# A transformer block on one core: the MLP's first product by 2 by 2 blocks with seven block products, token blocks in pairs

## The chip, the cores and the metric

The kernel runs on one core of a Trainium2 chip. The metric is the device time of one execution in microseconds (us), lower is better. Three runs of the kernel before took 2402.6, 2403.48 and 2406.64 us (median 2403.48).

The core's engines work side by side, each through its own instructions in the order of the program: TensorE (PE in the profile; PEld are its weight loads), VectorE (DVE), ScalarE (ACT), GpSimd (POOL) and SyncE (SP), which here issues all the DMAs.

## The reference

What is computed, cut to what matters (S = 2048 tokens, D = 576, 32 heads, F = 4608, all float32):

```python
x = A_x
mod = (_silu(c) @ w_mod).reshape(c.shape[0], 6, 1, -1)
sa, ca, ga, sb, cb, gb = (mod[:, 0], ..., mod[:, 5])
h = _layernorm(x) * (1 + ca) + sa
x = x + ga * _A_ref(h, A_wq, A_wk, A_wv, A_wo)     # 32 query heads, one k and v
h = _layernorm(x) * (1 + cb) + sb
y = _layernorm(h)
h = gelu(y @ w1 + b1)                              # [2048, 576] x [576, 4608]
x = x + gb * (h @ w2 + b2)                         # [2048, 4608] x [4608, 576]
```

## The kernel before

**Numbers.** Most matmuls take operands of type float32r, which keeps only part of a float32's bits. So each operand is split in two: hi is the value copied to float32r, lo is the value minus hi. A product is then three matmuls: hi by hi, hi by lo, lo by hi. The contraction over 576 rows has four blocks of 128 rows and a rest of 64. For the rest, the array has the 64 rows twice: the host stacks them, the lower copy is replaced by its lo part, and two matmuls with the hi and the lo of the other operand suffice. One block of 128 features by 512 tokens thus costs 4 x 3 + 2 = 14 matmuls of 512 columns.

**Stages.** The tokens lie in four blocks tb of 512, each of four tiles t of 128. Stage 1 makes q, k and v. Stage 2 runs the attention, 32 groups of four heads (n = 0 to 31, eight per token block), with the softmax's maxima, the scores, the exponentials and the product with V interleaved by a list written out by hand. A deque called fill holds generators for work on the side: the output projection of a block that is through (wo_block), its second layer norm (ln2_block). Each call of step(fill) runs one generator to its next yield. Stage 3 is the MLP. The instructions on each engine are in the order in which the Python code emits them; a yield is only a place at which the emitting code changes over to something else.

**Layer norm and operands.** ln2_tile (L513) normalizes one tile of 128 tokens, seven yields a tile in the MLP's first steps (blocks 2 and 3) and more in the attention (blocks 0 and 1). transpose_tile (L150) turns it over in PE into a psB buffer, ACT copies the hi part (L158) and DVE subtracts for the lo part (L159). The ten planes (five hi, five lo) of 128 x 512 lie in a tile Y[tb].

**MLP.** The features are in 18 groups of 256 (two blocks f of 128). A step is one group i and one token block tb. The list seq goes through the groups with blocks 0 and 1 for ten groups, with all four blocks for the eight others, then again through the first ten with blocks 2 and 3: 28 loads and splits of a group, 72 steps. Around a step:

- load_w (L733) loads W1's and W2's part of the group (640 and 576 KB); split_group (L743) splits them: ACT makes hi, POOL makes lo (DVE for the first groups) and multiplies W2 by half the gate. It yields between these pieces.
- fc1 (L763): per f the 14 matmuls into a psB buffer (proj, L232), then the GELU by its tanh form: ACT adds the bias (L776) and squares (L777), DVE multiplies (L778), ACT takes the tanh (L779), DVE multiplies (L781), ACT makes hi of the result, gh (L782), POOL its lo, gl (L783). It yields after the matmuls, after the tanh and at the end.
- fc2 (L786): per tile of 128 tokens 12 matmuls of 288 columns into one of two psA buffers, gh and gl standing, then DVE adds the result to XT (L802), which holds x and becomes the output.

The order within a step is the string "ma,tbt,sma,tbt,s": m and a are the matmuls and the first part of GELU, b its rest, t a tile of the second product of the step before, s a piece of split_group, and a comma a step of fill.

**Room.** psB has four buffers of one PSUM bank, psA two of two banks. The tag big has three buffers of 20 KB per partition (Y[0] to Y[2] and the attention's results in turn).

Of the kernel before, what the change touches and what calls it, by code (L numbers as in the profile page):

```python
# [15 lines left out]
NB = 4  # L16
TB = S // NB
NT = TB // 128
KD = 5
# [13 lines left out]
def block_kernel(ctx: ExitStack, tc, x, wqkv, wo, w1, b1, w2, b2, c, wmod, ident_in, out):  # L33
# [42 lines left out]
    pw = ctx.enter_context(tc.tile_pool(name="pw", bufs=1))  # L76
# [73 lines left out]
    def transpose_tile(Z, zt, t, k0, k1):  # L150
        p = psB()
        for k in range(k0, k1):
            tr(p[:, 128 * (k - k0):128 * (k - k0 + 1)], Z, k)
        n = k1 - k0
        src = p[:, :128 * n].rearrange("p (k c) -> p k c", k=n)
        hi = zt[:, k0:k1, 128 * t:128 * (t + 1)]
        lo = zt[:, KD + k0:KD + k1, 128 * t:128 * (t + 1)]
        ac.activation(hi, src, AF.Copy)  # L158
        ve.tensor_tensor(lo, src, hi.bitcast(F32), op=ALU.subtract)  # L159
# [325 lines left out]
    px = ctx.enter_context(tc.tile_pool(name="px", bufs=1, reuse_waits="tile"))  # L485
# [4 lines left out]
    WO, Y, ATT, B2 = {}, {}, {}, {}  # L490
# [22 lines left out]
    def ln2_tile(tb, t):  # L513
# [35 lines left out]
        transpose_tile(Z, Y[tb], t, 0, 4)  # L549
        yield  # L550
        transpose_tile(Z, Y[tb], t, 4, 5)
        yield

    def ln2_block(tb):
        if "b" not in B2:
            b2g = B2["b"] = px.tile([128, D], F32, name="b2g")
            sy.dma_start(b2g, b2.to_broadcast([128, D]))
            po.tensor_mul(b2g, b2g, BC[:, 2, :])
            po.tensor_scalar(b2g, b2g, 2.0, None, op0=ALU.mult)
        Y[tb] = big() if tb < 3 else pw.tile([128, 10, 512], F32R, name="y3", tag="wA", padded_shape=[128, 10, WQC])  # L560
        for t in range(NT):
            yield from ln2_tile(tb, t)

# [23 lines left out]
    def post_quad(n, PV):  # L587
# [23 lines left out]
        if qd < NQ - 1:  # L611
            for j in range(4):
                k, r = divmod(4 * qd + j, HC)
                sy.dma_start(A[DH * r:DH * (r + 1), :, k, :].bitcast(F32), os[32 * j:32 * j + DH].bitcast(F32))
        yield
# [69 lines left out]
    def between(n, kc):  # L685
# [8 lines left out]
        if kc == 1 and n >= 1 and n + 2 < NQT:  # L694
            load_q(n + 2)
        if kc == 8 and n % NQ == 0 and n:
# [28 lines left out]
    pv_mm(NQT - 1, 15, 0, 4)  # L725
    a2.__exit__(None, None, None)
# [4 lines left out]
    RAW, W, G = {}, {}, {}  # L731
    E = 10
    seq = [(i, (0, 1)) for i in range(E)] + [(i, (0, 1, 2, 3)) for i in range(E, NG)] + [(i, (2, 3)) for i in range(E)]  # L733
    final = {0: NG - 1, 1: NG - 1, 2: len(seq) - 1, 3: len(seq) - 1}

    def load_w(i):
        a = pm.tile([128, KD, 256], F32, name="w1r")
        b = pm.tile([128, 2, D], F32, name="w2r")
        sy.dma_start(a, w1[seq[i][0]])
        sy.dma_start(b, w2[seq[i][0]])  # L740
        RAW[i] = (a, b)

    def split_group(i):  # L743

        a, b = RAW.pop(i)
        h1 = pm.tile([128, KD, 256], F32R, name="w1h", bufs=2)
        l1 = pm.tile([128, KD - 1, 256], F32R, name="w1l", bufs=2)
        h2 = pm.tile([128, 2, D], F32R, name="w2h", bufs=2)
        l2 = pm.tile([128, 2, D], F32R, name="w2l", bufs=2)
        W[i] = (h1, l1, h2, l2)  # L750
        ac.activation(h1, a, AF.Copy)
        yield
        e = ve if i < 2 else po
        e.tensor_tensor(l1, a[:, :KD - 1], h1[:, :KD - 1].bitcast(F32), op=ALU.subtract)
        e.tensor_tensor(h1[64:, KD - 1], a[64:, KD - 1], h1[64:, KD - 1].bitcast(F32), op=ALU.subtract)
        yield
        (ve if i == 1 else po).tensor_tensor(b, b, BC[:, 2:3, :].to_broadcast([128, 2, D]), op=ALU.mult)
        yield
        ac.activation(h2, b, AF.Copy)
        po.tensor_tensor(l2, b, h2.bitcast(F32), op=ALU.subtract)  # L760
        yield

    def fc1(i, tb):  # L763

        h1, l1, _, _ = W[i]
        gh = pm.tile([128, 2, TB], F32R, name="gh", bufs=2)
        gl = pm.tile([128, 2, TB], F32R, name="gl", bufs=2)
        G[i, tb] = (gh, gl)
        for f in range(2):
            p = psB()  # L770
            proj(p, h1, l1, 128 * f, 128 * (f + 1), Y[tb])
            yield
            ft = 2 * seq[i][0] + f
            h = pm.tile([128, TB], F32, name="gx", bufs=2)
            s = px.tile([128, TB], F32, name="gs", tag="OT"[f])
            ac.activation(h, p, AF.Identity, bias=b1t[:, ft:ft + 1])  # L776
            ac.activation(p, p, AF.Square, bias=b1t[:, ft:ft + 1])  # L777
            ve.scalar_tensor_tensor(s, p, 1.0 / GA3, h, op0=ALU.add, op1=ALU.mult)  # L778
            ac.activation(p, s, AF.Tanh, scale=GC * GA3)  # L779
            yield  # L780
            ve.scalar_tensor_tensor(h, p, 1.0, h, op0=ALU.add, op1=ALU.mult)  # L781
            ac.activation(gh[:, f, :], h, AF.Copy)  # L782
            po.tensor_tensor(gl[:, f, :], h, gh[:, f, :].bitcast(F32), op=ALU.subtract)  # L783
            yield

    def fc2(i, tb):  # L786
        _, _, h2, l2 = W[i]
        gh, gl = G.pop((i, tb))
        for t in range(NT):
            p = psA()  # L790
            ts_ = slice(128 * t, 128 * (t + 1))
            for nn in range(2):
                cs = slice(288 * nn, 288 * (nn + 1))
                terms = []
                for f in range(2):
                    terms += [(gh[:, f, ts_], h2[:, f, cs]), (gh[:, f, ts_], l2[:, f, cs]),
                              (gl[:, f, ts_], h2[:, f, cs])]
                for q, (a, b) in enumerate(terms):
                    pe.matmul(p[:, nn, :288], a, b, start=(q == 0), stop=(q == len(terms) - 1))  # L799
            X = XT[:, NT * tb + t, :]  # L800
            Xv = X.rearrange("p (a b) -> p a b", a=2)
            ve.tensor_tensor(Xv, p[:, :, :288], Xv, op=ALU.add)  # L802
            if i == final[tb]:
                r0 = TB * tb + 128 * t
                sy.dma_start(out[r0:r0 + 128, :], X)
            yield

    load_w(0)
    wop = {(t, h2): (psC if t == 3 and h2 else psM if t < 2 and t + h2 < 2 else psB)()
           for t in range(NT) for h2 in range(2)}  # L810
    for t in range(NT):
        for h2 in range(2):
            wo_mm(NB - 1, t, h2, wop[t, h2], 0, KD - 1)
    for gen in posts:
        drain(gen)
    drain(split_group(0))
    for t in range(NT):
        for h2 in range(2):
            wo_mm(NB - 1, t, h2, wop[t, h2], KD - 1, KD)
            wo_add(NB - 1, t, h2, wop[t, h2])  # L820
    open_ps("3", 4)
    load_w(1)
    fill = deque([ln2_block(2), ln2_block(3)])
    steps = [(i, tb) for i in range(len(seq)) for tb in seq[i][1]]
    prev = None
    sp = iter(())
    for e, (i, tb) in enumerate(steps):
        if tb == seq[i][1][0]:
            drain(sp)
            W.pop(i - 2, None)  # L830
            if i + 1 < len(seq):
                sp = split_group(i + 1)
        if tb == 2:
            while fill:
                step(fill)
        f1 = fc1(i, tb)
        f2 = fc2(*prev) if prev else iter(())
        order = "ma,tbt,sma,tbt,s"
        if e == 0:
            order = "masbmab"  # L840
        elif e == 1:
            order = "mabmttsabtts"
        elif e == len(steps) - 1:
            order = "mabm,a,tbttt"
        for o in order:
# [56 lines left out]
```

## Time and profile before

| | |
|---|---|
| median of three runs | 2403.48 us |
| the profiled execution | 2401.06 us |
| its span | 2399.2 us |
| PE, DVE, ACT, POOL busy, share of the span | 98%, 71%, 71%, 32% |
| first matmul of the MLP | 1448.84 us |
| granted clock of PE | 0.999 |

The span is the time from the first to the last instruction that the profiler recorded. "Busy" is the time in which an engine executes; waiting is not counted. In lists of instructions the columns are start, length, engine, line, operation, out<-in, shapes, and in brackets the idle time just before with what ended it. In lists of groups they are line, engine, operation, count, then the busy time in us, the mean length in ns, and the idle time in front.

### The profile page before, as it was taken

To read this page: it belongs to the slowest core of one execution; us is meant where nothing else is said; L and a number is where in the kernel's file an instruction comes from. 1 tells how busy PE (TensorE), PEld (TensorE's weight loads), DVE (VectorE), ACT (ScalarE), POOL (GpSimd) and SP (SyncE) were. 2 spreads that over 40 slices of the span, in tenths; PEclk is the share of its full clock that TensorE was granted. 3 is DMA by queue.
4 is the path that set the end of the run, shared out by engine and by line. 5 is a ranking of instruction groups with operands and counts; after the bars stand their busy time and mean duration, and the time that the engine had idled before them with its cause. 6 is when DMAs were issued, how large, how long until landed. Compare 5 with 4: busy or idle time off the path is not lost.

```text
span 2399.2 us, 42867 instructions
## 1 busy us (share of the span) xinstructions
PE 2356.6 (98%) x16802; PEld 1492.0 (62%) x16802; DVE 1712.5 (71%) x3069; ACT 1691.8 (71%) x3170; POOL 766.4 (32%) x669
## 2 busy tenths in 40 slices
PE   8999999999999999999999999999999999999999
PEld 6643444454444444444544348888899899989988
DVE  6589999979999889999799926767444444444444
ACT  5469999979999889999799994444444444444443
POOL 6502211114331123321010113665543333345553
PEclk9999999999999999999999999999999999999999
DMA  6412000000000000000000001111100000011111
GB/s 216 139 64 71 18 23 22 14 19 22 19 21 19 17 19 22 19 22 14 14 22 19 18 28 53 42 52 42 53 22 31 21 22 22 26 67 52 44 52 50
DMA packets 40586, 91.86 MB, mean 38 GB/s; under 512 B 5835, under 2 KB 9547, under 8 KB 40385
## 3 DMA queue, kind: packets, MB, share of 16 engines
q1 hardware_dynamic: 40385, 89.13, 11.6%
q8 instruction: 132, 2.16, 0.4%
q14 instruction: 69, 0.57, 0.1%
HBM read 66.06 MB, written 14.16 MB: 33 GB/s over the span
## 4 chain that ended last, share of the span: by engine, by line
PE 87%; DVE 6%; ACT 4%; issue 1%; POOL 1%; DMA 1%; SPq 0%; POOLq 0%; ACTq 0%; DVEq 0%
PE psC L650 20%; PE psB L239 20%; PE psA L799 17%; PE psB L661 10%; PE psM L310 10%; PE psB L671 4%; PE psB L573 2%; ACT P L663 2%; DVE mx L683 1%; PE psB L148 1%; PE psA L310 1%; PE psB L194 1%; DVE XT L802 1%; DVE Z L532 1%; ACT O L592 0%
## 5 line engine op out<-in xcount | busy, mean ns | idle before, releaser
L663 ACT ACTIVATE P<-psB 128x512 f32<-128x512 f32 x2048 | 1049.9, 617 | 2.2 <-PE psB L661 1.1
L683 DVE TENSOR_REDUCE mx<-psM 128x1 f32<-128x512 f32 x1476 | 943.1, 683 | 47.5 <-PE psM L310 27.3
L650 PE MATMUL psC<-P,V 128*32 128x256 f32 (+1 forms) x6056 | 598.2, 466 | 12.1 <-ACT O L592 12.1
L310 PE MATMUL psM<-KS,qst 64*128 64x512 f32 x1722 | 596.9, 432 | 3.3 <-DVE mx L683 2.4
L661 PE MATMUL psB<-qst,KS 64*128 64x512 f32 x2048 | 598.0, 433 | 1.0 <-DMA qst<-ms 0.5
L778 DVE SCALAR_TENSOR_TENSOR gs<-psB,gx 128x512 f32<-128x512 f32 x144 | 99.6, 692 | 453.3 <-ACT psB L777 453.3
L661 PEld LDWEIGHTS psB<-qst,KS 64*128 64x128 f32 x2048 | 305.0, 184 | 166.5 <-issue 72.5
L310 PEld LDWEIGHTS psM<-KS,qst 64*128 64x128 f32 x1722 | 284.3, 184 | 127.7 <-DVE mx L681 79.5
L783 POOL TENSOR_TENSOR gl<-gx,gh 128x512 fp32r<-128x512 f32 x144 | 188.6, 1309 | 494.1 <-ACT gh L782 447.3
L799 PE MATMUL psA<-w2h,gl 128*128 128x288 f32 x1152 | 341.4, 296 | 3.2 <-POOL gl L783 3.2
L799 PE MATMUL psA<-w2h,gh 128*128 128x288 f32 x1152 | 340.2, 295 | 1.9 <-ACT gh L782 1.5
L799 PE MATMUL psA<-w2l,gh 128*128 128x288 f32 x1152 | 340.0, 295 | 0.0
L239 PE MATMUL psB<-big,w1h 128*128 128x512 f32 x1080 | 338.5, 395 | 0.2 <-DVE XT L577 0.2
L776 ACT ACTIVATE gx<-psB,b1t 128x512 f32<-128x512 f32 x144 | 98.8, 686 | 251.6 <-PE psB L239 247.2
L650 PEld LDWEIGHTS psC<-P,V 128*32 128x32 f32 x6056 | 119.6, 108 | 230.3 <-issue 207.1
L239 PEld LDWEIGHTS psB<-big,w1h 128*128 128x128 f32 x1080 | 196.9, 188 | 41.0 <-issue 0.5
L799 PEld LDWEIGHTS psA<-w2h,gh 128*128 128x128 f32 x1152 | 216.2, 188 | 9.6 <-ACT gh L782 2.2
L799 PEld LDWEIGHTS psA<-w2l,gh 128*128 128x128 f32 x1152 | 216.5, 188 | 5.6
L799 PEld LDWEIGHTS psA<-w2h,gl 128*128 128x128 f32 x1152 | 216.2, 188 | 4.6 <-POOL gl L783 4.6
L802 DVE TENSOR_TENSOR XT<-psA,XT 128x576 f32<-128x576 f32 x288 | 214.9, 747 | 5.5 <-PE psA L799 5.5
L674 ACT ACTIVATE xc<-psB 128x512 f32<-128x512 f32 x246 | 147.7, 600 | 88.2 <-PE psM L310 69.7
L782 ACT ACTIVATE gh<-gx 128x512 fp32r<-128x512 f32 x144 | 91.1, 633 | 154.2 <-DVE gx L781 154.2
(151 smaller groups left out, 2616.6 us busy)
## 6 DMA issues: line engine op xcount, KB each, us to landing
w1r<-in_w SPq DMA_DIRECT2D x28, 640.0 KB
w2r<-in_w SPq DMA_DIRECT2D x28, 576.0 KB
qst<-qscr SPq DMA_DIRECT2D x192, 72.0 KB
qscr<-qs SPq DMA_DIRECT2D x16, 504.0 KB
big<-os SPq DMA_DIRECT2D x112, 72.0 KB
bigw<-in_wmod SPq DMA_DIRECT2D x5, 1440.0 KB
out<-XT SPq DMA_DIRECT2D x16, 288.0 KB
XT<-in_x SPq DMA_DIRECT2D x3, 1152.0 KB
```

Source lines behind the costliest of these rows:

```text
L239: pe.matmul(o, a, b, start=(i == 0), stop=(i == len(terms) - 1))
L310: pe.matmul(o, QST[n][64 * g:64 * g + 64, p, 128 * qt:128 * (qt + 1)], KS[64 * g:64 * g + 64, 512 * kb:512 * (kb + 1)], start=True, stop=True)
L650: pe.matmul(PVt[n][32 * j:32 * (j + 1), cs], V[:, kc, :], t[:, j, cs], start=(kc == 0 and h0 == 0), stop=(kc == 15), skip_group_check=True)
L661: pe.matmul(t, KS[64 * g:64 * g + 64, 128 * kc:128 * (kc + 1)], QST[n][64 * g:64 * g + 64, i, :], start=True, stop=True)
L663: ac.activation(P[n, kc][:, 2 * i + g, :], t, AF.Exp, scale=SCALE)
L674: ac.activation(XC[-1], t, AF.Relu)
L683: ve.tensor_reduce(o, t, axis=AX.X, op=ALU.max)
L776: ac.activation(h, p, AF.Identity, bias=b1t[:, ft:ft + 1])
L778: ve.scalar_tensor_tensor(s, p, 1.0 / GA3, h, op0=ALU.add, op1=ALU.mult)
L783: po.tensor_tensor(gl[:, f, :], h, gh[:, f, :].bitcast(F32), op=ALU.subtract)
L799: pe.matmul(p[:, nn, :288], a, b, start=(q == 0), stop=(q == len(terms) - 1))
L802: ve.tensor_tensor(Xv, p[:, :, :288], Xv, op=ALU.add)
```

## The change

Call A11, A12 (feature block 0) and A21, A22 (feature block 1) the blocks of a group's W1 by pairs of 128 rows, and B11, B21, B12, B22 the operand's blocks by the same pairs of rows and by two token blocks. The four results C = A B would need eight block products of six matmuls (two row blocks, three terms each). The change takes Winograd's form of Strassen's scheme with seven: sums S1 to S4 of blocks of A and T1 to T4 of blocks of B are formed first, and the products are put together through U: A11 B11 (into ba), S2 T2 (bb), S3 T3 (bc), A12 B21 (onto ba), S1 T1 (bd), A22 T4 (onto bc), S4 B22 (onto bd). The rests of 64 rows come on top as eight matmuls.

- A round v is one group and one pair of token blocks: 36 rounds, all 18 groups for blocks 0 and 1, then for 2 and 3. Each round loads and splits its W1 and W2 part anew.
- The sums T are formed once for each pair: in the layer norm's end (T2, on POOL), at the attention's end and in round 17 (op_pieces). transpose_tile keeps the plain float32 value instead of hi and lo.
- The sums S, their hi and lo are formed in each round for the next one, on DVE, ACT and POOL (w1_sum, w1_sum_lo, w1_a, w1_22, w1_tails), into one set of planes W1["r"] and from one raw tile W1["a"]. The first set is formed in the last head group of the attention (first_split).
- w2_split handles one half of W2 with no yield inside: multiply, copy, subtract; on POOL, in round 0 on DVE.
- GELU has three pieces with yields (gens, g_), one for each of the four results, and fc2 goes over the eight tiles of a pair, in the round after.

The diff, cut to what is spoken of here:

```diff
-    def transpose_tile(Z, zt, t, k0, k1):
+    def transpose_tile(Z, yr, t, k0, k1, e):
...
-        ac.activation(hi, src, AF.Copy)
-        ve.tensor_tensor(lo, src, hi.bitcast(F32), op=ALU.subtract)
+        dst = yr[:, k0:k1, 128 * t:128 * (t + 1)]
+        if e is ac:
+            ac.activation(dst, src, AF.Copy)
+        else:
+            ve.tensor_copy(dst, src)
...
+    def w1_hi(a, n, src):
+        ac.activation(W1["r"][:, a:a + n], src, AF.Copy)
+
+    def w1_lo(a, n, src, e):
+        e.tensor_tensor(W1["r"][:, 17 + a:17 + a + n], src, W1["r"][:, a:a + n].bitcast(F32), op=ALU.subtract)
+
+    def w1_a(e=po):
+        src = W1["a"][:, :KD - 1, 0, :]
+        w1_hi(0, 4, src)
+        w1_lo(0, 4, src, e)
...
+    SUMS = {4: "S2", 6: "S3", 10: "S1", 12: "S4"}
+
+    def w1_sum(a):
+
+        o = W1["s"]
+        def op(x, y, how):
+            ve.tensor_tensor(o, x, y, op=how)
+        if SUMS[a] == "S3":
+            op(w1_raw(0, 0), w1_raw(1, 0), ALU.subtract)
+        elif SUMS[a] == "S4":
+            op(w1_raw(0, 1), W1["r"][:, 4:6].bitcast(F32), ALU.subtract)
+            op(o, W1["r"][:, 21:23].bitcast(F32), ALU.subtract)
+        else:
+            op(w1_raw(1, 0), w1_raw(1, 1), ALU.add)
+            if SUMS[a] == "S2":
+                op(o, w1_raw(0, 0), ALU.subtract)
+        w1_hi(a, 2, o)
+
+    def w1_sum_lo(a):
+        w1_lo(a, 2, W1["s"], ve)
...
+    def w2_split(v, f, e):
+
+        (h, l), o = W2[v % 2], W2R[f]
+        e.tensor_tensor(o, o, BC[:, 2, :], op=ALU.mult)
+        ac.activation(h[:, f], o, AF.Copy)
+        e.tensor_tensor(l[:, f], o, h[:, f].bitcast(F32), op=ALU.subtract)
+
+    def product(o, w, b, first=True, tail=None):
+
+        h, l = W1["r"][:, w:w + 2], W1["r"][:, 17 + w:19 + w]
+        terms = []
+        for k in range(2):
+            terms += [(h[:, k], OP[:, b + k]), (h[:, k], OP[:, 14 + b + k]), (l[:, k], OP[:, b + k])]
+        if tail:
+            wt = W1["r"][:, 14 + tail[0]]
+            terms += [(wt, TL[0][:, tail[1]]), (wt, TL[0][:, 2 + tail[1]])]
+        for i, (x, y) in enumerate(terms):
+            pe.matmul(o, x, y, start=(first and i == 0), stop=(i == len(terms) - 1), skip_group_check=True)
...
+    def gelu(v, f, b, p):
...
+        ac.activation(h, p, AF.Identity, bias=b1t[:, ft:ft + 1])
+        ac.activation(p, p, AF.Square, bias=b1t[:, ft:ft + 1])
+        yield
+        ve.scalar_tensor_tensor(s, p, 1.0 / GA3, h, op0=ALU.add, op1=ALU.mult)
+        ac.activation(p, s, AF.Tanh, scale=GC * GA3)
+        yield
+        ve.scalar_tensor_tensor(h, p, 1.0, h, op0=ALU.add, op1=ALU.mult)
+        ac.activation(GT[:, 2 * u], h, AF.Copy)
+        po.tensor_tensor(GT[:, 2 * u + 1], h, GT[:, 2 * u].bitcast(F32), op=ALU.subtract)
...
+    def t_():
+        next(f2, None)
+
+    def g_():
+
+        for gen in list(gens):
+            if next(gen, 0) == 0:
+                gens.remove(gen)
+
+    load_w2(0)
+    for v in range(NV):
+        nx = v + 1 < NV
+        e2 = po if v else ve
...
+        ba = psB()
+        product(ba, 0, 0)
+        ac.activation(U[:, 0], ba, AF.Copy)
+        t_()
+        g_()
+        more("+B11 -B11")
+        bb = psB()
+        product(bb, 4, 6)
+        ve.tensor_tensor(U[:, 0], bb, U[:, 0], op=ALU.add)
+        t_()
+        g_()
+        w2_split(v, 0, e2)
+        more("+T2")
+        bc = psB()
+        product(bc, 6, 10)
+        ve.tensor_tensor(U[:, 1], bc, U[:, 0], op=ALU.add)
+        if nx:
+            w1_sum(4)
+        more("-T2 =T3")
+        t_()
+        if nx:
+            w1_sum_lo(4)
+        product(ba, 2, 2, False, (0, 0))
+        gens.append(gelu(v, 0, 0, ba))
+        g_()
+        if nx:
+            w1_a()
+            w1_sum(6)
+        more("+T3 +B21 -B21")
+        t_()
+        w2_split(v, 1, e2)
+        if nx:
+            w1_sum_lo(6)
+            load_w2(v + 1)
+        g_()
+        bd = psB()
+        product(bd, 10, 8, True, (1, 1))
+        be = psB()
+        ve.tensor_tensor(be, bd, U[:, 1], op=ALU.add)
+        g_()
+        gens.append(gelu(v, 1, 1, be))
+        g_()
+        if nx:
+            w1_sum(10)
+        more("-T3 =T4 =T1 +T1")
+        t_()
+        if nx:
+            w1_sum_lo(10)
+        g_()
+        product(bc, 8, 12, False, (1, 0))
+        ve.tensor_tensor(bc, bc, U[:, 0], op=ALU.add)
+        g_()
+        gens.append(gelu(v, 1, 0, bc))
+        g_()
+        if nx:
+            w1_22()
+        more("-T1 +T4 +t0 -t0")
+        t_()
+        g_()
+        product(bd, 12, 4, False, (2, 1))
+        ve.tensor_tensor(bd, bd, U[:, 0], op=ALU.add)
+        g_()
+        gens.append(gelu(v, 0, 1, bd))
+        g_()
+        t_()
+        if nx:
+            w1_sum(12)
+            w1_tails()
+            w1_sum_lo(12)
+        more("-T4 +B22 -B22 +t1 -t1")
         drain(f2)
...
+        f2 = fc2(v)
+        if v + 2 < NV:
+            load_w1((v + 2) % NG)
```

In rounds 1 to 16 more() runs one step of fill (the layer norm of blocks 2 and 3), in round 17 it forms operands of the second pair. Per round that is, on PE, 50 matmuls of 512 columns and 96 of 288.

More of the change, by code (lines that the diff above doesn't have):

```diff
@@ L725, in block_kernel @@
     pv_mm(NQT - 1, 15, 0, 4)
+    while fill:
+        step(fill)
     a2.__exit__(None, None, None)
@@ new lines, in block_kernel, with load_w2 @@
+    open_ps("3", 4)
+    w1_rooms()
+    load_w1(1)
+    GT = big()
+    U = px.tile([128, 2, TB], F32, name="u")
+    W2R = [px.tile([128, D], F32, name="w2r", bufs=2) for _ in range(2)]
+    W2 = [px.tile([128, 2, D], F32R, name="w2s", bufs=3) for _ in range(3)]
+    W2.append(W1["r"][:, 31:40].rearrange("p a b -> p (a b)").rearrange("p (f c) -> p f c", f=2))
+    W2 = W2[:2], W2[2:]
+    B2.clear()
+    NV = 2 * NG
+    def load_w2(v):
+        for f in range(2):
+            sy.dma_start(W2R[f], w2[v % NG, :, f, :])
@@ L759, in split_group @@
[L759 to L784, printed above, removed]
@@ L795, in fc2 @@
                 for f in range(2):
[L796 to L800, printed above, removed]
+                    gh, gl = (GT[:, 2 * G[v, b, f] + l, ts_] for l in range(2))
+                    terms += [(gh, h2[:, f, cs]), (gh, l2[:, f, cs]), (gl, h2[:, f, cs])]
@@ L821, in block_kernel @@
[L821 to L833 removed]
+    fill = deque([ln2_block(2), ln2_block(3)])
+    f2 = iter(())
+    gens = deque()
+    def t_():
+        next(f2, None)
```

205 lines of the change are left out of this document (130 added, 75 removed).

## The prediction

> **What bounds the kernel now.** I read the page's engine shares first, then the stages as windows, then the matmuls of one step in order of time.
>
> ```profile
> span 2399.2 us, 42867 instructions
> PE 2356.6 (98%) x16802; PEld 1492.0 (62%) x16802; DVE 1712.5 (71%) x3069; ACT 1691.8 (71%) x3170; POOL 766.4 (32%) x669
> ```
>
> ```profile
> 1449.00:2399.00 950.00, 937.84 (x5512) 841.51 (x5511) 463.65 (x684) 419.67 (x646) 434.39 (x289) 1.00 0.12 40
> 1700.00:2300.00 600.00, 600.00 (x3535) 540.84 (x3534) 252.13 (x372) 263.43 (x403) 245.48 (x154) 1.00 0.11 36
> ```
>
> The columns after the window and its length are PE, PE's weight loads, DVE, ACT, POOL, the granted clock and DMA. The share of 71% for DVE and ACT comes from the attention and says nothing about the MLP, which fills 1449 to 2399. There PE is busy 937.84 of 950 us, in the 600 us from 1700 on all of the time and at clock 1.00, while DVE, ACT and POOL work 42%, 44% and 41%. So today PE sets the MLP's time, and the others have more than half of it free. The next view is PE alone in order of time (start, length).
>
> ```profile
> 1901.18 0.29 PE L799 MATMUL psA<-w2h,gh 128*128 128x288 f32 x1
> ...
> 1904.38 0.63 PE L239 MATMUL psB<-big,w1h 128*128 128x512 f32 x2
> ...
> 1907.64 0.29 PE L799 MATMUL psA<-w2h,gh 128*128 128x288 f32 x1
> ```
>
> A matmul's own length overlaps its neighbours; what counts is start to start. Two tiles of the second product, 24 matmuls, run from 1901.18 to 1904.38: 0.133 us each. One feature block of the first product, 14 matmuls, runs from 1904.38 to 1907.64: 0.233 us each. A step (group, token block) has 28 and 48: 6.52 + 6.40 = 12.92 us. Two steps, which are what one round of the changed kernel replaces, take 25.84 us, and 36 such pairs 930 us.
>
> **What the change removes.** Per round (a group, a pair of blocks) seven products of six matmuls and eight tail matmuls stand for 56: 50, so 6 x 0.233 = 1.40 us go, and PE's own work is 24.44 us. Over 36 rounds that is 50.3 us, the whole possible gain. (The Trainium skill, "TensorE: Matmul & The Clock Gate", section "Back-to-back issue gap", gives about 131 ns for a sustained 512-column matmul; by that the 216 matmuls would be worth 28 us. This trace disagrees with 233 ns, and the measurement decides.)
>
> **What it adds, and where.** ACT, DVE and POOL each execute their own instructions in the order of the program, so I follow one round through them. The prices come from one GELU of before, in order of time:
>
> ```profile
> 1901.44 0.69 ACT L776 ACTIVATE gx<-psB,b1t 128x512 f32<-128x512 f32 x1 [1.34 <-PE psB L239]
> 1902.03 0.65 ACT L777 ACTIVATE psB<-psB,b1t 128x512 f32<-128x512 f32 x1
> 1902.72 0.69 DVE L778 SCALAR_TENSOR_TENSOR gs<-psB,gx 128x512 f32<-128x512 f32 x1 [3.67 <-ACT psB L777]
> 1903.44 0.60 ACT L779 ACTIVATE psB<-gs 128x512 f32<-128x512 f32 x1 [0.76 <-DVE gs L778]
> 1904.15 0.69 DVE L781 SCALAR_TENSOR_TENSOR gx<-psB,gx 128x512 f32<-128x512 f32 x1
> 1904.76 0.75 DVE L802 TENSOR_TENSOR XT<-psA,XT 128x576 f32<-128x576 f32 x1
> 1904.87 0.63 ACT L782 ACTIVATE gh<-gx 128x512 fp32r<-128x512 f32 x1 [0.83 <-DVE gx L781]
> ...
> 1905.58 1.30 POOL L783 TENSOR_TENSOR gl<-gx,gh 128x512 fp32r<-128x512 f32 x1 [2.53 <-ACT gh L782]
> ```
>
> From the bias step to the end of gl it is 5.44 us over four engines' hand-overs; queued instructions of one engine start 0.59 (ACT) and 0.61 (DVE) apart. And from these groups by size, and one DVE instruction of 256 columns:
>
> ```profile
> L547 POOL TENSOR_TENSOR XT<-XT,b2g 128x576 f32<-128x576 f32 x8 | 11.8, 1477 | 0.1
> L759 ACT ACTIVATE w2h<-w2r 128x1152 fp32r<-128x1152 f32 x27 | 31.1, 1151 | 3.7 <-DVE w2r L757 2.6 <-POOL w2r L757 1.1
> L158 ACT ACTIVATE big<-psB 128x512 fp32r<-128x512 f32 x4 | 2.3, 581 | 0.0
> L158 ACT ACTIVATE big<-psB 128x128 fp32r<-128x128 f32 x4 | 1.0, 259 | 0.0
> L754 DVE TENSOR_TENSOR w1l<-w1r,w1h 128x1024 fp32r<-128x1024 f32 x1 | 1.2, 1218 | 0.0
> ```
>
> ```profile
> 1467.30 0.42 DVE L755 TENSOR_TENSOR w1h<-w1r,w1h 64x256 fp32r<-64x256 f32 x1
> ```
>
> By width: an ACT copy of 256 columns is about 0.37, of 576 about 0.65 (between 0.58 and 1.15); a DVE step of 256 columns 0.42; a POOL step of 576 about 1.42.
>
> Busy time per round is not the trouble. ACT: four GELUs 9.7, the copies of weights and sums 4.5, U 0.6: 15 us. DVE: 13 steps of 512 columns (eight of GELU, five sums of products) 8, eight additions to XT 5.3, eleven steps on weights 4.7: 18 us. POOL: four gl 5.2, two halves of w2 at two steps each 5.7, lo parts and tails 3: 14 us. All lie under 24.44. The trouble is the order. Call the GELUs A, B, C, D as they come; the last step of each is issued before the first of the next, so they don't overlap. A second thing is new: the two halves of w2 are split in one go, so that ACT's copy waits at the head of its queue for a POOL multiplication, which itself stands behind another POOL step. Before, a yield separated the two. The loop, from the end of A's square to the same point a round later, in us:
>
> - ACT copies W1's rows 0.60, POOL forms their lo 1.37, POOL multiplies w2's second half 1.41, ACT copies it 0.72: 4.10. A's tanh is queued behind that copy.
> - A's tanh 0.57, DVE 0.79, copy 0.66: 6.12.
> - B: bias and square 1.13, copy of S1 0.36, its lo on DVE 0.46 (ahead of B's DVE step), DVE 0.63, tanh 0.64, DVE 0.79, copy 0.66: 10.8.
> - C: 1.2, 0.7, 0.65, 0.8: 14.15.
> - D's DVE step stands behind an XT addition 0.66, two steps of S4 0.88, the wait for ACT's copy of it 0.41, its lo 0.45 and two XT additions 1.32; with its own 0.62: 18.5. Its second stands behind a sum of products and an XT addition: 1.9, copy 0.66: 21.06.
> - POOL: D's gl 1.37, then w2's first half 1.4, ACT's copy 0.7, the copy of S2 0.36, the next A's bias and square 1.2: 26.1.
>
> So with no contention at all the loop takes 26.1 us, 1.7 more than PE's work and 0.3 more than the 25.84 of before. What is late next, beside it: PE waits at the first tile of the second product for C's gl, and at the seventh for a psA buffer, since the XT additions are queued in the same DVE order.
>
> Contention comes on top. DVE (two SBUF inputs) and POOL in order of time:
>
> ```profile
> 1503.88 0.76 DVE L531 TENSOR_TENSOR Z<-Z,BC 128x576 f32<-128x576 f32 x1
> ...
> 1525.69 1.74 DVE L531 TENSOR_TENSOR Z<-Z,BC 128x576 f32<-128x576 f32 x1
> 1527.47 3.10 DVE L532 TENSOR_TENSOR Z<-Z,BC 128x576 f32<-128x576 f32 x1
> ```
>
> ```profile
> 1525.25 1.56 POOL L783 TENSOR_TENSOR gl<-gx,gh 128x512 fp32r<-128x512 f32 x1 [1.01 <-ACT gh L782]
> 1526.78 3.17 POOL L760 TENSOR_TENSOR w2l<-w2r,w2h 128x1152 fp32r<-128x1152 f32 x1
> ```
>
> The same step takes 0.76 alone; at 1525.69 it lasts until 0.6 us after gl ends, POOL's next step is stretched meanwhile, and DVE's next lasts until POOL's ends: 3.10. They take turns. The new round has eleven such DVE steps among 14 us of POOL work. On the loop lie the second step of S4 behind C's gl (1.3), w2's first half behind a step of S2 (0.45) and its second half behind S3's lo (0.45), with 0.4 of smaller ones: 0 to 2.6; I take 2.0, since the three named meet by the order itself. The round is then 28.1 us. (The Trainium skill, "SBUF — State Buffer", section "Who interferes with whom", calls this an exclusive lock: a DVE instruction with two SBUF inputs and a GpSimd one that reads SBUF block each other for the whole instruction. The trace agrees, 3.10 against 0.76. Without the rule the round would be 26.1.)
>
> Unknown prices. DVE now writes PSUM, which no row shows; ACT's write to PSUM (0.65 at 1902.03) is no dearer than its write to SBUF (0.69), so 0.69, from 0.6 to 1. W1 is loaded into one buffer, after the tails are formed; w1 and w2 of before were issued at 1413.77 and 1414.36:
>
> ```profile
> 1413.77 0.47 SPq L739 DMA_DIRECT2D w1r<-in_w  x1
> 1414.36 0.36 SPq L740 DMA_DIRECT2D w2r<-in_w  x1
> ...
> 1418.99 2.65 POOL L757 TENSOR_TENSOR w2r<-w2r,BC 128x1152 f32<-128x1152 f32 x1 [8.58 <-DMA w2r<-in_w]
> ```
>
> Both (1216 KB) had landed 5.2 us after the first issue, so 640 KB need at most that and about 4; S2 is wanted some 4 after the issue. At 5.2, DVE waits 1.2, half of it where POOL's turn would have stopped it anyway: 0 to 1, inside the range. The DMA issues stand on SP alone, behind which nothing but the next loads waits.
>
> **The rest of the MLP.** The layer norm of blocks 2 and 3 rides on rounds 1 to 8, one tile each.
>
> ```profile
> L532 DVE TENSOR_TENSOR Z<-Z,BC 128x576 f32<-128x576 f32 x8 | 12.8, 1606 | 0.3
> L531 DVE TENSOR_TENSOR Z<-Z,BC 128x576 f32<-128x576 f32 x8 | 10.4, 1301 | 0.3
> L543 DVE TENSOR_SCALAR Z<-Z,mv,rs 128x576 f32<-128x576 f32 x8 | 9.9, 1242 | 0.0
> L529 DVE TENSOR_SCALAR Z<-XT,mv,rs 128x576 f32<-128x576 f32 x8 | 9.0, 1130 | 0.0
> L544 DVE COPY Z<-Z 128x64 f32<-128x64 f32 x8 | 8.0, 1006 | 0.3
> ```
>
> These are 6.3 us of DVE a tile, hidden today under a DVE that is 42% busy; in a loop that runs through DVE part of it shows: 0 to 50 us for eight tiles, I take half, 25. Forming the operands of the second pair in round 17 is eight DVE steps of 1024 columns (1.22 each: 9.8) and 8 us of ACT: 0 to 18, I take 10. Before the first round the same forms share DVE and ACT with the attention's last additions:
>
> ```profile
> 1448.84 0.70 PE L239 MATMUL psB<-big,w1h 128*128 128x512 f32 x2 [0.25 <-DVE XT L577]
> 2386.29 0.63 ACT L782 ACTIVATE gh<-gx 128x512 fp32r<-128x512 f32 x1 [0.83 <-DVE gx L781]
> ```
>
> PE has the output projection's matmuls until then, so I take 2 us later than 1448.8 (0 to 9.8). The attention itself is unchanged and PE's: the smaller transposes and the first weight split hide there. The first round lacks the second product's additions, 24 us; the last lacks the weight sums, 25. Today 12.9 us follow the last gh at 2386.29, of which four tiles are 6.4; eight tiles are 12.8, so 12.9 + 6.4, or 19.
>
> Sum of the span: 1448.8 + 2 + 24 + 34 x 28.1 (955.4) + 25 + 19 + 25 + 10 = 2509.2 us. The profiled run of before was 2401.06 us, 1.9 over its span, and the median 2403.48 another 2.4 over that: 2513.5, say 2513 us, 4.6% slower.
>
> **The rivals.** *PE stays the bound*, if the queues slide over each other more than I read: 1448.8 + 2 + 24 + 35 x 24.44 (855.4) + 19 + 8 (what the layer norm may cost PE today: 950 - 937.84 is 12, less the ends) = 2357, with 4.3 on top 2361 us, 1.8% faster. For it: busy sums of 15, 18 and 14 us under 24.44. Against it: 26.1 us of steps in a row, none of them PE's. It decides as soon as the loop is shorter than 24.44. *Loop and old step even out*: no contention and a hidden layer norm, 34 x 26.1 = 887 in the sum, 2441 with all extras and 2404 with none; near 2403 only with none. *DVE becomes the bound by blocking*: each of the eleven steps waits half a POOL step (0.7), 18 + 7.7 + waits for ACT of 5 or so, 31 us a round: 2610 us. For it the 3.10 row; against it, that POOL works only half of the round. *It doesn't do what it says*: 50 matmuls a round are counted from the code, so no chance.
>
> **How the numbers follow.** A measurement of this kernel can tell about 0.2% (5 us; the three runs span 4). Loop-bound as summed 0.67, its own range 2408 to 2570 us (loop 26.1 without extras, to 28.7 with a start 8, layer norm 45 and forms 18); blocking 0.08; even 0.05; PE-bound 0.20. Slower 0.75, same 0.05, faster 0.20. The time is the likeliest's, 2513; the range goes up to 2600 for most of the blocking case and down to 2390 for the even one, leaving the PE-bound one out, which is 2 in 10.
>
> **What would show it.** PE busy about 87% in the middle of the MLP, with 24.4 of 28 us; its waits named as POOL's gl and the XT additions; ACT's wait for POOL's w2 multiplication near 2.8 us twice a round; S4's second step near 1.7 us instead of 0.42; rounds 1 to 8 longer than the later ones. Wrong would be PE at 99% in the rounds after 18, or a round under 25.8 us.

## The result and the profile after

The changed kernel takes 2520.58 us (median of four runs, 2520.07 to 2521.1) against 2403.38 us: ratio 1.0485, interval 1.0467 to 1.0503, slower by 4.9%. The forecast was 2513 us. The profiled execution has a span of 2518.3 us.

First the page's shares, then two windows of the MLP (window, length, then busy time of PE, its weight loads, DVE, ACT, POOL, granted clock, DMA).

```profile
span 2518.3 us, 43839 instructions
PE 2351.6 (93%) x16586; PEld 1468.0 (58%) x16586; DVE 2080.7 (83%) x3644; ACT 1791.9 (71%) x3512; POOL 902.6 (36%) x860
```

```profile
1520.00:1720.00 200.00, 168.99 (x924) 146.68 (x924) 164.12 (x273) 90.44 (x174) 108.43 (x106) 0.94 0.13 40
...
2000.00:2400.00 400.00, 362.31 (x2099) 318.20 (x2099) 308.77 (x462) 203.27 (x391) 213.38 (x174) 1.00 0.17 52
```

PE has 216 matmuls less and yet is no longer the bound: from 2000 to 2400 it works 91% of the time, where before it worked all of the time from 1700 to 2300. No other engine is full either: DVE 77%, ACT 51%, POOL 53%. That is the picture of a loop of waits and not of a full engine. Who waited for whom in the MLP (total us, times, longest):

```profile
ACT w2s L906 <- POOL w2r L905: 200.3, 70, 5.4
...
PE psA L954 <- DVE XT L958: 86.5, 63, 6.5
...
PE psA L954 <- POOL big L939: 15.6, 33, 0.6
```

ACT's copy of each half of W2 waits for POOL's multiplication 200.3 / 70 = 2.9 us, twice a round. One round shows why. ACT in order of time, from the bias step of GELU A (L931) to the same step a round later:

```profile
2209.30 0.67 ACT L931 ACTIVATE gx<-psB,b1t 128x512 f32<-128x512 f32 x1
...
2214.12 0.69 ACT L906 ACTIVATE w2s<-w2r 128x576 fp32r<-128x576 f32 x1 [2.32 <-POOL w2r L905]
2214.71 0.58 ACT L935 ACTIVATE psB<-gs 128x512 f32<-128x512 f32 x1
2216.12 0.63 ACT L938 ACTIVATE big<-gx 128x512 fp32r<-128x512 f32 x1 [0.83 <-DVE gx L937]
...
2232.42 0.63 ACT L938 ACTIVATE big<-gx 128x512 fp32r<-128x512 f32 x1 [1.83 <-DVE gx L937]
2236.25 0.69 ACT L906 ACTIVATE w2s<-w2r 128x576 fp32r<-128x576 f32 x1 [3.19 <-POOL w2r L905]
2236.84 0.40 ACT L649 ACTIVATE w1a<-w1s 128x256 fp32r<-128x256 f32 x1
2237.14 0.67 ACT L931 ACTIVATE gx<-psB,b1t 128x512 f32<-128x512 f32 x1
```

A's tanh (2214.71) has had its input since DVE's step of 2212.71, 0.68 us long, but is queued behind W2's second half, which waits 2.32 us; the next A's bias step is queued behind the first half, which waits 3.19 us. The producer of that first half is late itself: POOL multiplies only when it is through with D's lo part.

```profile
2212.71 0.68 DVE L934 SCALAR_TENSOR_TENSOR gs<-psB,gx 128x512 f32<-128x512 f32 x1
```

```profile
2233.19 1.43 POOL L939 TENSOR_TENSOR big<-gx,big 128x512 fp32r<-128x512 f32 x1 [4.01 <-issue]
2234.58 1.63 POOL L905 TENSOR_TENSOR w2r<-w2r,BC 128x576 f32<-128x576 f32 x1
```

The round is 2237.14 - 2209.30 = 27.84 us. Blocking between DVE and POOL shows too, here S4's two subtractions (DVE) and C's lo part (POOL):

```profile
2225.23 0.41 DVE L669 TENSOR_TENSOR w1s<-w1r,w1a 128x256 f32<-128x256 f32 x1
2225.68 1.38 DVE L669 TENSOR_TENSOR w1s<-w1s,w1a 128x256 f32<-128x256 f32 x1
```

```profile
2225.39 1.39 POOL L939 TENSOR_TENSOR big<-gx,big 128x512 fp32r<-128x512 f32 x1 [1.75 <-ACT big L938]
```

The first takes 0.41; the second has the same shape, lies under POOL's step and ends 0.3 us after it.

Round lengths from one copy of U (L993) to the next, counted from round 0: 25.7 for round 0, 36.2 for round 1, 30.3 to 33.7 for rounds 2 to 8, 32.7 for round 9, 27.8 for the quiet ones (10 to 16, and 19 on), 42.6 for round 17.

### The profile page after: what moved, and what is told of

It reads as the page before. It is cut to its first block, busy times and chain, and to the rows that moved or that the text cites. A ratio compares the mean times of both kernels' runs of the same rounds, so it can differ in the third digit from the quotient of the medians.

```text
span 2518.3 us, 43839 instructions
## 1 busy us (share of the span) xinstructions
PE 2351.6 (93%) x16586; PEld 1468.0 (58%) x16586; DVE 2080.7 (83%) x3644; ACT 1791.9 (71%) x3512; POOL 902.6 (36%) x860
## 4 chain that ended last, share of the span: by engine, by line
PE 52%; ACT 15%; DVE 14%; POOL 10%; issue 7%; DMA 1%; SPq 0%; DVEq 0%; POOLq 0%; ACTq 0%
PE psC L750 19%; PE psB L761 10%; PE psM L312 9%; POOL w2r L905 4%; PE psB L771 4%; DVE gx L937 3%; ACT P L763 3%; DVE w1s L669 2%; ACT psB L935 2%; PE psB L241 2%; PE psA L954 2%; ACT gx L931 2%; PE psB L584 2%; ACT psB L932 2%; POOL big L939 2%
## 5 line engine op out<-in xcount | busy, mean ns | idle before, releaser
L954 PE MATMUL psA<-w2s,big 128*128 128x288 f32 x2880 | 529.8, 304 | 113.4 <-DVE XT L958 86.5
L954 PEld LDWEIGHTS psA<-w2s,big 128*128 128x128 f32 x2880 | 445.9, 193 | 160.3 <-DVE XT L958 56.5
L919 PE MATMUL psB<-ops,w1a 128*128 128x512 f32 x1512 | 401.6, 402 | 8.4 <-DVE psB L1029 5.1
L939 POOL TENSOR_TENSOR big<-gx,big 128x512 fp32r<-128x512 f32 x144 | 194.9, 1354 | 332.9 <-ACT big L938 198.9
L919 PEld LDWEIGHTS psB<-ops,w1a 128*128 128x128 f32 x1512 | 276.2, 192 | 57.9 <-DVE psB L1029 5.7
L938 ACT ACTIVATE big<-gx 128x512 fp32r<-128x512 f32 x144 | 90.9, 631 | 160.1 <-DVE gx L937 160.1
L906 ACT ACTIVATE w2s<-w2r 128x576 fp32r<-128x576 f32 x72 | 49.4, 686 | 205.1 <-POOL w2r L905 200.3
L652 DVE TENSOR_TENSOR w1a<-w1s,w1a 128x256 fp32r<-128x256 f32 x144 | 103.2, 717 | 100.2 <-ACT w1a L649 88.7
L954 PE MATMUL psA<-w1a,big 128*128 128x288 f32 x576 | 171.5, 298 | 0.0
L781 DVE CUSTOM_DVE_ANT_0 xc<-psM,xc 128x512 f32<-128x512 f32 x246 | 167.3, 680 | 0.0
L935 ACT ACTIVATE psB<-gs 128x512 f32<-128x512 f32 x144 | 86.1, 598 | 109.4 <-DVE gs L934 109.4
```

The source lines that it names most:

```text
L781: ve.tensor_tensor_reduce(c, t, c, 1.0, -3.0e38, ALU.add, ALU.max, o)
L919: pe.matmul(o, x, y, start=(first and i == 0), stop=(i == len(terms) - 1), skip_group_check=True)
L939: po.tensor_tensor(GT[:, 2 * u + 1], h, GT[:, 2 * u].bitcast(F32), op=ALU.subtract)
L954: pe.matmul(p[:, nn, :288], x, y, start=(q == 0), stop=(q == len(terms) - 1))
```

## The experiments

All times are compared with 2520.6 for the changed kernel unless another is named; the kernel before, in the same sessions, took 2402.1 to 2404.5. Round lengths are taken between the same lines as above.

**W2's multiplications early.** Both are issued at the end of the round before.

```diff
-        e.tensor_tensor(o, o, BC[:, 2, :], op=ALU.mult)
+        if v == 0:
+            e.tensor_tensor(o, o, BC[:, 2, :], op=ALU.mult)
...
             w1_sum_lo(12)
+            for f in range(2):
+                po.tensor_tensor(W2R[f], W2R[f], BC[:, 2, :], op=ALU.mult)
```

> The two POOL multiplications of W2 for the next round are issued together at the end of a round, where POOL is free, so that ACT's copies no longer wait for them; nothing is left out. Changed kernel: 2520.6 us, a round 27.8. Chain theory (the round is a loop of steps in the queues of ACT, DVE and POOL): the first ACT copy starts about 3.0 us earlier, of which S2's second step lets 1.6 through; the second copy frees 1.3: a round near 24.9 us, the whole near 2420. Rival, DVE is the bound through blocking: the same DVE and POOL steps remain, so at most 0.9 us a round, 2490 or more. Rival, PE is the bound (lower granted clock, psA buffers): no change, 2520.

Measured: 2436.49 us, a quiet round 25.35. No step was taken away from any engine, only their order changed, and 84 us went. The wait of ACT for POOL was most of the loss; PE as the bound and DVE's blocking as the bound are both refuted. Nor did the new order gain by less blocking: by the means of their groups from 2000 to 2400, DVE's steps on the weights took 7.5 us a round in place of 7.8. It fell short of 2420: the round kept 0.45 us more than worked out, because the loop now closes through PE. A's bias step no longer stands behind W2 but waits for the fourth block product:

```profile
2225.10 0.69 ACT L932 ACTIVATE gx<-psB,b1t 128x512 f32<-128x512 f32 x1 [0.51 <-PE psB L920]
```

**GELUs overlapped.** The first piece of B, C and D is issued ahead of the last piece of the one before.

```diff
-        g_()
-        gens.append(gelu(v, 1, 1, be))
+        gens.appendleft(gelu(v, 1, 1, be))
         g_()
```

> The first piece of each next GELU (bias, square on ACT) is issued before the last piece of the one before; nothing is left out. Chain theory: each of three hand-overs is shortened by about 1.4 us (the wait for DVE and the copy), 4.1 a round, more than the 3.4 that PE leaves, so a round near 24.6 us and the whole near 2410 to 2425. DVE blocking: no step is taken away, 2510 or more. PE bound: 2520.

Measured: 2504.64 us, a round 27.33 and not 24.6. The theory failed here, and the trace says where. ACT, then POOL:

```profile
2211.32 0.69 ACT L931 ACTIVATE gx<-psB,b1t 128x512 f32<-128x512 f32 x1 [0.56 <-POOL big L939]
2211.91 0.65 ACT L932 ACTIVATE psB<-psB,b1t 128x512 f32<-128x512 f32 x1
2212.47 0.63 ACT L938 ACTIVATE big<-gx 128x512 fp32r<-128x512 f32 x1
```

```profile
2213.18 1.27 POOL L939 TENSOR_TENSOR big<-gx,big 128x512 fp32r<-128x512 f32 x1 [1.20 <-ACT big L938]
```

D's bias step waits for one of two gx buffers and now stands ahead of C's copy, so C's lo part starts late, at 2213.18. The second product's first tile needs it, and the additions to XT of that tile and the next stand ahead of D's own DVE steps:

```profile
2215.74 0.76 DVE L958 TENSOR_TENSOR XT<-psA,XT 128x576 f32<-128x576 f32 x1 [0.34 <-PE psA L954]
...
2218.72 0.76 DVE L958 TENSOR_TENSOR XT<-psA,XT 128x576 f32<-128x576 f32 x1 [0.82 <-PE psA L954]
2219.39 0.68 DVE L937 SCALAR_TENSOR_TENSOR gx<-psB,gx 128x512 f32<-128x512 f32 x1
```

So this part of the loop goes through PE. From A's bias step to C's last DVE step the trace has 13.36 us in place of 14.66, a gain of 1.3; from there to D's last DVE step 8.53 in place of 7.75, so D gave 0.8 back. And the 1.3 is less than half of the 2.8 that two hand-overs promised, in part because S1's lo (DVE) now meets A's lo part (POOL) and takes 1.31 or 1.32 in place of 0.43 (here a round later):

```profile
2232.86 1.32 DVE L652 TENSOR_TENSOR w1a<-w1s,w1a 128x256 fp32r<-128x256 f32 x1
```

```profile
2232.60 1.29 POOL L939 TENSOR_TENSOR big<-gx,big 128x512 fp32r<-128x512 f32 x1 [0.76 <-ACT big L938]
```

The same trace also tests the blocking: with C's lo part at 2213.18, S4's steps before it run free.

```profile
2212.13 0.41 DVE L669 TENSOR_TENSOR w1s<-w1r,w1a 128x256 f32<-128x256 f32 x1
2212.58 0.42 DVE L669 TENSOR_TENSOR w1s<-w1s,w1a 128x256 f32<-128x256 f32 x1
2212.92 0.28 DVE L688 TENSOR_TENSOR w1d<-w1r 128x128 f32<-128x128 f32 x1
2213.55 1.19 DVE L652 TENSOR_TENSOR w1a<-w1s,w1a 128x256 fp32r<-128x256 f32 x1 [0.34 <-ACT w1a L649]
```

The second is 0.42 in place of 1.38, and the step that now meets POOL, S4's lo, takes 1.19 instead of 0.42 to 0.43.

**PE's tail matmuls left out.** The products then lack their rest of 64 rows.

```diff
-        if tail:
+        if False:
             wt = W1["r"][:, 14 + tail[0]]
```

> Leaves out the eight tail matmuls of every round (the rest of 64 rows): 8 x 0.233 = 1.86 us of PE less in each of 36 rounds. Chain theory: PE isn't on the loop at these places, so at most 0.3 us a round, 2510 to 2520. PE bound: 36 x 1.86 = 67 us less, 2454. DVE blocking: no change, 2520.

Measured: 2522.91 us, a round 27.83. Taking 1.86 us of matmuls out of every round gains nothing; from 2000 to 2400 PE is busy 349 of 400 us where it was busy 362.

**The lo parts of the sums left out.** The four calls in a round are deleted, so that the lo parts of the first group are used throughout; one of the four:

```diff
-        if nx:
-            w1_sum_lo(4)
         product(ba, 2, 2, False, (0, 0))
```

> Leaves out the four DVE steps a round that form the lo parts of the sums S1 to S4 (those of the first group are used throughout): 4 x 0.72 us of DVE. Chain theory: of the four only S1's (about 0.7) and S4's (about 0.65) stand on the loop, with 0.2 of blocking: 1.5 us a round, 2465 to 2470. DVE blocking as the bound: all 2.9 us a round, 2420. PE bound: no change, 2520.

Measured: 2488.93 us, a round 26.93: 0.9 us for 2.9 us of DVE work. DVE's occupancy is not the bound. It is also less than the 1.5 of the chain theory, for the reason of the second experiment: S4's lo stands in a part where the way through PE is about as long. Without it DVE reaches the addition to XT of the second tile sooner and waits there 0.82 us for PE, where it waited 0.48.

**The layer norm's pieces aligned.**

```diff
             except StopIteration:
                 q.popleft()
+                if al:
+                    step(q, al)
```

> A step of the side work runs on into the next generator where one ends, so that the seven pieces of every layer norm tile stand at the same seven places of a round; before, the change from block 2 to block 3 used up one place and moved all of block 3's pieces by one (rounds 5 to 8 took 33.3 to 33.7 us, rounds 2 to 4 30.3). Theory, a layer norm tile costs what the place of its pieces in the queues makes it: rounds 5 to 8 fall to about 30.3 and the whole by 13 to 16 us, to about 2506. Rival, the pieces cost their DVE time wherever they stand (or block 3 is dearer for the lower granted clock): rounds 5 to 8 stay at 33.5, 2520.

Measured: 2506.55 us, as expected. Round 6 from one copy of U to the next, first of the changed kernel, then of this one:

```profile
1635.25 0.59 ACT L993 ACTIVATE u<-psB 128x512 f32<-128x512 f32 x1
1668.91 0.59 ACT L993 ACTIVATE u<-psB 128x512 f32<-128x512 f32 x1
```

```profile
1635.05 0.58 ACT L995 ACTIVATE u<-psB 128x512 f32<-128x512 f32 x1
1665.30 0.57 ACT L995 ACTIVATE u<-psB 128x512 f32<-128x512 f32 x1
```

33.66 against 30.25 us for the same instructions one place earlier.

**D's pieces within the round,** with the early W2 and alone.

```diff
         gens.append(gelu(v, 0, 1, bd))
         g_()
         t_()
+        g_()
...
         drain(f2)
+        g_()
```

> The early W2 multiplications (2436.5 us, a round 25.35), and the second and third pieces of a round's last GELU issued within the round instead of after the next round's first and second tile of the second product. Theory, the part of the loop from the third GELU to the end of the fourth goes through PE (its lo part, the first tile, two block products, the second tile): with this GELU ahead of them the round falls to PE's own 24.4 to 24.7 us, the whole to about 2410. Rival, DVE's occupancy holds the round: no DVE step is taken away, 25.3 stays, 2436.

> The changed kernel with only the last GELU's second and third pieces moved into the round. Theory: the way from the third GELU's last DVE step to the fourth's (7.75 us in the trace) falls by about 1.9 us, a round near 25.9 and the whole near 2455, although no engine has less to do. Rival, DVE's occupancy or PE: 2515 to 2520.

Measured: 2445.24 us with a round of 25.86 (with the early W2; 8.8 us more than without this step), and 2493.7 with 27.09 (alone; 27 less than the changed kernel). Both miss. ACT and PE of the first of the two:

```profile
2205.28 0.67 ACT L932 ACTIVATE gx<-psB,b1t 128x512 f32<-128x512 f32 x1
...
2215.91 0.67 ACT L932 ACTIVATE gx<-psB,b1t 128x512 f32<-128x512 f32 x1
```

```profile
2203.12 1.56 PE L920 MATMUL psB<-ops,w1a 128*128 128x512 f32 x6
2204.52 0.63 PE L920 MATMUL psB<-opt,w1a 128*128 128x512 f32 x2
...
2221.37 0.53 PE L955 MATMUL psA<-w2s,big 128*128 128x288 f32 x2 [0.37 <-POOL big L940]
```

A's bias step starts at once after the fourth block product (2203.12 to 2204.99). A, B and C follow one behind the other, C starting at 2215.91, until C's lo part frees the first tile at 2221.37; from there PE has two block products, their tiles and the next round's fourth product. 16.4 us of GELUs and 9.5 us of PE make 25.86.

D is not on this loop, and it was not on it in the first experiment either, where A already waited for the fourth block product; so moving D could not shorten it. It lengthened PE's part, which had taken 8.8 us (2216.01 to 2224.84 in the first experiment's trace): D's first DVE step, which waits 1.16 us for ACT, now stands ahead of an addition to XT, and PE waits for that addition.

```profile
2221.11 0.69 DVE L935 SCALAR_TENSOR_TENSOR gs<-psB,gx 128x512 f32<-128x512 f32 x1 [1.16 <-ACT psB L933]
...
2223.48 0.75 DVE L959 TENSOR_TENSOR XT<-psA,XT 128x576 f32<-128x576 f32 x1
```

```profile
2224.28 0.40 PE L955 MATMUL psA<-w2s,big 128*128 128x288 f32 x1 [0.30 <-DVE XT L959]
```

Alone, moving D did shorten the loop, by 0.74 us a round of the 1.9 forecast; then, there too, A's bias step waited for the fourth block product (1.45 us idle before it).

**All three together,** with b2 loaded early.

```diff
     load_w2(0)
+    b2g = B2["b"] = px.tile([128, D], F32, name="b2g")
+    sy.dma_start(b2g, b2.to_broadcast([128, D]))
```

> All three of these (early W2 multiplications, last GELU within the round, aligned layer norm pieces), and the load of b2 and its two POOL steps ahead of the first layer norm tile. Theory: 2410 less about 15 for the alignment and 5 for b2, 2390. If the costs don't add because PE becomes the bound, 2400 to 2405; rival DVE occupancy: 2420 or more.

Measured: 2452.73 us, the same round of 25.86; the aligned places, which gained 14 us in the changed kernel, cost here (30.5 us in rounds 5 to 8 against 28.4 to 29.1 in the run before it with the early W2). The costs don't add.

**Two overlaps.** The loop just read is shortened where it is long: B's and C's first pieces ahead, D's left where it is, with the early W2, b2 loaded early and, from the second round on, D within the round.

```diff
-        g_()
-        gens.append(gelu(v, 1, 0, bc))
+        gens.appendleft(gelu(v, 1, 0, bc))
         g_()
```

> The early W2 multiplications and the last GELU within the round (2445.2 us together, a round 25.86), and now the second and third GELU's first pieces ahead of the last piece of the one before; b2 loaded early. In the trace of the two together the round is a loop that goes through PE: the fourth block product, GELUs one to three in a row (16.3 us to the third's lo part), then the first tile of the second product, two block products and their tiles (9.1) back to it. Theory: two hand-overs of 1.4 us less make that loop 23 us, PE's own 24.4 is then the bound, a round 24.4 to 24.7, the whole 2400 to 2410. Rival, the sum of DVE's busy time and its blocking holds the round at 25.3 or more: 2430 to 2445.

Measured: 2407.43 us, ratio to the kernel before 1.0017 (interval 1.0007 to 1.0026), a quiet round 24.73. The window from 2000 to 2400 now reads:

```profile
2000.00:2400.00 400.00, 397.83 (x2380) 356.78 (x2379) 332.46 (x505) 220.01 (x422) 223.09 (x188) 1.00 0.16 50
```

PE is busy 99.5%: it is the bound again, at 24.73 where its own work was put at 24.44, with the same instructions in another order. The round fell as far as the loop was shortened, until PE stopped it; this confirms the loop as the cause of the quiet rounds' length. It is the best version found, about level with the kernel before.

**The layer norm moved or spread.** Rounds 1 to 9 of that version, which have the layer norm, still take 40 us more than quiet ones (262.4 - 9 x 24.73). Three attempts on top of it. A tile's normalizing steps, multiplication, addition and copy on POOL:

```diff
-        fine = tb < 2
+        fine = True
```

The two normalizing steps and the small copy on ACT, with a bias of -mean x rs that POOL forms (cut to the first):

```diff
-        (po if fine else ve).tensor_scalar(h, X, mv[:, 0:1], rs, op0=ALU.subtract, op1=ALU.mult)
+        if fine:
+            po.tensor_scalar(h, X, mv[:, 0:1], rs, op0=ALU.subtract, op1=ALU.mult)
+        else:
+            ac.activation(h, X, AF.Identity, scale=rs, bias=nb)
```

One piece at every second place, without the empty one:

```diff
             if 0 < v < NG - 1:
-                step(fill)
+                cnt[0] += 1
+                if cnt[0] % 2:
+                    step(fill)
```

> The same with the layer norm of blocks 2 and 3 on POOL in nine pieces a tile, as blocks 0 and 1 have it, so that DVE has about 3.5 us a tile instead of 8.8 and POOL about 7 instead of 1.5. Theory, the extra time of the layer norm rounds comes from its pieces in DVE's queue: rounds 1 to 9 fall from about 30 to 26 or 27, 20 to 30 us less than the run without it. Rival, POOL's pieces stand ahead of the lo parts and block DVE's steps on the weights just as long: no gain, or 5 to 20 us more.

> The version with two overlaps (2407.4 us; rounds 10 on 24.7, rounds 1 to 9 28 to 29, where DVE is busy nearly throughout), with the two normalizing steps and the small copy of a layer norm tile of blocks 2 and 3 on ACT instead of DVE. Theory, in these rounds DVE's queue is the bound: 1.8 us of DVE steps and about 0.9 of its wait for POOL's reciprocal root go, rounds 1 to 9 fall to 26 to 27, the whole by 15 to 22 us, to 2385 to 2392, below both kernels. Rival, the new ACT steps stand ahead of GELU's in ACT's queue and wait there for POOL: no gain or a loss, 2405 to 2415.

> The version with two overlaps (2407.4 us), with the layer norm of blocks 2 and 3 spread over rounds 1 to 16, one piece at every second place and without the piece that issues nothing. In the quiet rounds DVE is busy 85% of 24.7 us, so 3.7 us are free; a tile needs about 6 without blocking. Theory, a round of the layer norm is long because a whole tile's DVE steps don't fit into what DVE has free: half a tile a round nearly fits, rounds 1 to 16 come to 25 to 26.3, 8 to 24 us of extra in place of about 40, the whole 2385 to 2398, below both kernels. Rival, every piece delays the queue where it stands, however many a round: the sum stays, 2405 to 2410.

Measured: 2440.73, 2416.16 and 2420.98 us. All are dearer than 2407.43, and the rounds with the layer norm cost 72, 48 and 54 us more than quiet ones. On POOL, DVE waits for it (over 1475 to 1800):

```profile
DVE bst L137 <- POOL Z L535: 41.5, 8, 7.4
```

On ACT, PE's transposes wait for ACT over the MLP, 23.7 us, where they waited 9.8 for DVE:

```profile
PE psB L149 <- ACT Z L558: 23.7, 8, 3.2
```

At half rate rounds 2 to 16 scatter between 25.2 and 31.6; that this goes by where the pieces happen to fall is likely but was not traced. In each case DVE had less to do a round, and it did not help. All three theories missed. The rivals had the direction, but the loss was larger than they allowed: 33 us on POOL where they had at most 20, 2416 on ACT where they had up to 2415, and 14 us at half rate where they had the sum unchanged.

## Why the prediction was right, and where it was off

By its own terms, with rounds as measured in the changed kernel:

- **PE's own work, 24.44 us a round, and a possible gain of 50.3.** Right: with the order mended a round is 24.73 at 99.5% busy. Beside the 25.84 of before that is 1.1 us a round, 40 us, and it is more than spent on the layer norm (40) and round 17 (11). So the gain was there and was not realized.
- **The round, 28.1 us by a loop through ACT, DVE and POOL.** 27.83 measured. The two W2 waits in it are shown by the first experiment; PE and DVE's occupancy are excluded by the third and fourth. ACT's wait was forecast at 2.8 us twice a round and is 2.9. PE's 24.44 of 27.83 us are 88%, forecast at about 87%; the profile's busy share, 91%, is higher.
- **Blocking between DVE and POOL.** The rows agree, 1.38 against 0.41 (1.7 was forecast), and the second experiment's trace shows the step free when POOL is elsewhere. How much of the 2.0 us that I took lies on the loop was not tried by itself, since it can't be taken away without moving other steps. So this term is argued and not shown.
- **"None of them PE's" failed.** The steps of D were worked out as a pure queue on DVE. In the trace two ways of nearly the same length lead there: DVE's queue, and the one by C's lo part, the first tile, the next block product and the second tile. PE waits for C's lo part, and DVE, 0.48 us early, waits for PE ahead of D's last step:

```profile
2226.83 0.53 PE L954 MATMUL psA<-w2s,big 128*128 128x288 f32 x2 [0.48 <-POOL big L939]
```

```profile
2231.03 0.76 DVE L958 TENSOR_TENSOR XT<-psA,XT 128x576 f32<-128x576 f32 x1 [0.48 <-PE psA L954]
2231.71 0.68 DVE L937 SCALAR_TENSOR_TENSOR gx<-psB,gx 128x512 f32<-128x512 f32 x1
```

That the sum came out right although the path was wrong here is luck: the two ways were nearly equal. The forecasts of the second and fourth experiments came out too large in part for the same reason. Those for moving D missed because, once W2 is early or D is moved, the loop closes through PE's fourth block product, which the prediction did not have on it at all.
- **Layer norm, 25 us.** 43.9 measured (294.4 for rounds 1 to 9, less 9 x 27.83), within the 0 to 50 stated. I had taken half; 14 to 16 of the missing 19 are the slip of one place at the change of blocks (the aligned run), which I had not seen: a step of fill that only ends a generator uses up a place.
- **Round 17, 10 us.** 14.8. **First round, 24 us.** 25.7. Both have the forms or splits in the same queues; which wait carried the difference was not traced.
- **The start, 2 us later than 1448.8.** It was 1.6 earlier:

```profile
1447.24 4.94 PE L919 MATMUL psB<-ops,w1a 128*128 128x512 f32 x20 [0.44 <-DVE XT L588]
```

The forms hid under the output projection. **The last round and the tail, 44 us**, were 41.5 (2518.3 less 2476.8, where the last round's first product began). Together: 1447.2 + 25.7 + 946.2 + 43.9 + 14.8 - 0.9 (round 18) + 41.5 = 2518.4; the forecast of the span was 2509.2. The errors of 19 and 5 up partly cancelled those of 9, 4 and 2.5 down, so the closeness of the total, 2520.58 against 2513, owes something to luck too. One sum in the prediction is incomplete: the rival in which loop and old step even out was given as 2441 and 2404 without the 4.3 us that the other sums add from span to median.

What stays open: why the layer norm's 40 us resist all of three moves. That it depends on the places is shown; which of the waits in a given round carries it was not traced through.

## What to carry to other kernels

When work is taken from a bound engine, add up the others' steps not only as busy time but once around the loop of a round, through each queue in its order; here ACT, DVE and POOL were busy 14, 21 and 15 us a round (forecast 15, 18 and 14), PE 24.4, and the loop took 27.8. Look first for an instruction whose input another engine has only just been given: issue the producer a stage earlier. And where two paths are nearly tied, shortening one shows next to nothing, so reread the trace after each step.

## What the runs showed of the hardware that was not expected

- The granted clock fell where PE's waits were longer: 0.83 from 1460 to 1490 with waits of 4.35 and 4.43 us, 0.94 from 1520 to 1720 with waits of 2.8 and 3.8, and 1.00 from 2000 to 2400, where none is over 1.6. Without the tails no wait listed from 2000 to 2400 is over 2.3 us, and the mean was 0.96. It cost nothing that could be seen there: that run's quiet round, with eight matmuls less, is 27.83 us like the changed kernel's.

```profile
1460.00:1490.00 30.00, 20.22 (x90) 16.84 (x90) 19.03 (x30) 11.21 (x22) 15.11 (x14) 0.83 0.13 42
```

- DVE writes PSUM as fast as SBUF: 0.68 us for 512 columns from PSUM and SBUF into PSUM, and 0.68 for the same operation into SBUF. The prediction had no row for this and took 0.69.

```profile
2213.31 0.68 DVE L1029 TENSOR_TENSOR psB<-psB,u 128x512 f32<-128x512 f32 x1
2229.87 0.68 DVE L999 TENSOR_TENSOR u<-psB,u 128x512 f32<-128x512 f32 x1
```
